# A transformer block on one core: all 32 output-projection groups in one row, and the order of small work around them

## The chip, the core and the metric

The kernel runs on one core of one Trainium2 chip. A core has five engines that run their own instruction streams and wait for each other through semaphores: TensorE (PE; its weight loads are listed as PEld), VectorE (DVE), ScalarE (ACT), GpSimd (POOL) and SyncE (SP), whose queue issues nearly all DMA transfers here. The metric is the time of one execution in microseconds of device time; lower is better. Matmuls write to PSUM, which has eight banks; DVE and ACT read the results out of it.

## What is computed

One pre-LN transformer block on a sequence of 2048 tokens of width 1024: layer norm, sliding-window attention (32 heads of width 32, window 256), output projection with residual, a second layer norm, and an MLP of width 3584 with SiLU, again with residual.

```python
def _A_ref(x, wqkv, wo):
    H = 32; Dh = D // H; W = 256
    q, k, v = ...                       # x @ wqkv, split by head
    scores = jnp.einsum("bhqd,bhkd->bhqk", q, k) * (Dh ** -0.5)
    mask = (idx[:, None] - idx[None, :] >= 0) & (idx[:, None] - idx[None, :] < W)
    p = _softmax(jnp.where(mask[None, None], scores, -1e9))
    o = jnp.einsum("bhqk,bhkd->bhqd", p, v)
    return o.transpose(...).reshape(B, S, D) @ wo

def _B_ref(x, w1, w2):
    return jnp.einsum("bsf,fd->bsd", _silu(jnp.einsum("bsd,df->bsf", x, w1)), w2)

h = x + _A_ref(_layernorm(x), A_wqkv, A_wo)
h2 = h + _B_ref(_layernorm(h), B_w1, B_w2)
```

All inputs are bf16; sums are kept in float32.

## The kernel before

The tokens are cut into four blocks of 512 (`NB` = 4), a block into four tiles of 128. The order of all instructions is written out by hand, and each engine runs its own in that order. The unit of dense work on TensorE is a group: eight matmuls of 128x128 weights against 512 columns that add up in one PSUM bank, the accumulator, which DVE (sometimes ACT) then reads out. While attention is running, three accumulators rotate (`next_acc`, `acc_n`, the first three of `four`); the fourth bank, `o_ps`, holds the outputs of attention, and four more banks, `sc`, hold scores.

The stages, by dense groups:

- Block 0's value groups, then its 16 query and key groups (`qk_group`).
- Blocks 1, 2 and 3: 24 groups each (8 value, 16 query and key), with the first layer norm of the next block between them.
- The row (L691 to L714): 24 groups of the output projection (`wo_group`), two column halves for each of four tiles of blocks 0, 1 and 2.
- The MLP (from L741), for each block 28 groups of the first product (`h1_group`, then `silu` with a tanh on ACT and a multiply on DVE) and then the second product (`mm2`). Block 0's first product holds the remaining eight groups of the output projection, block 3's, one behind each of its groups 7 to 14 (L751).

Attention is not a stage of its own. It is woven into the dense groups by `Attention.between`, which `qk_group`, `v_group` and `wo_group` call ahead of each of their eight matmuls. It counts these calls (`seen`), and at certain counts it issues either a visit (the score matmuls for some heads, with the exponentials on ACT and the causal and window masks on POOL) or a piece (`attn_piece`: 24 matmuls of 128x33 into `o_ps`, L419, then `attn_norm`: a reciprocal, L430, and a multiply, L431, on DVE, which divide by the softmax sums and free `o_ps`). From block 1 on, twelve periods of 48 counts handle two units of four heads each, i and i+1: visits at 4, 20 and 36 counts, pieces at 41, 46, 59 and 76 counts behind the period's start. The pieces at 41 and 46 are the two halves of unit i, and stand five dense matmuls apart in one group. A third visit (`visit(i, 2)`) writes to `sc`, to `o_ps` and to the accumulator of the group before. With the row's first group at count 704, the last period starts in the row's group 10, and its last piece comes in group 19.

When a unit's second half is done, its transposition by DMA into `qT` goes to `late` and is issued on SP at the next group's start (`run_late`). `wo_group` for a block reads `qT` of that block; it adds the residual (`r_in`, six buffers, loaded by `load_res`) on DVE (L285) into one of two buffers `t_out`, and the store of a finished tile to `h_dram` goes to `late` as well. A tile's two adds must wait until the store of the tile two before has left its buffer.

Block 0's second layer norm is made in the row (`ln2_steps(0)`): one load of 1 MB back from `h_dram` (L623, behind group 9), then 16 steps, in this order: four of statistics (two halves L193 and an aggregate L201 each), a first guess and three Newton rounds for the inverse root (L209 to L216), two normalizations (L221), and then transpositions by DMA (L225) and the other two normalizations in turn. One step follows each of groups 11 to 13, and two follow each group from 14 on, until none is left. The first MLP product of block 0 reads all four transpositions.

The row also issues the loads of the MLP's first weights (`load_w1`). The second weights (`load_w2`) are loaded into regions that the attention used: one at the MLP's start, five more in program order behind group 4 of the first product, and the last one behind its end.

At the MLP's start, the banks of `sc` become four more accumulators, so that seven rotate from there on; `acc_n` is set so that the next accumulator is the one that was used longest ago.

Of the kernel before, what the change touches and what calls it, by code (L numbers as in the profile page):

```python
# [47 lines left out]
def kernel(  # L48
# [21 lines left out]
    NB = S // 512  # L70
# [168 lines left out]
    acc_n = [0]  # L239
    acc_banks = [b[:] for b in four]  # L240

    def next_acc():
        acc_n[0] += 1
        return acc_banks[acc_n[0] % len(acc_banks)]
# [24 lines left out]
    def load_res(t):  # L269
        nc.sync.dma_start(out=r_in[t % 6], in_=x2d[t * P:(t + 1) * P, :])  # L270
# [3 lines left out]
    def run_late():  # L274
        while late:
            late.pop(0)()

    def wo_group(b, j, c, between=None):
        acc = next_acc()
        for g in range(G):  # L280
            if between:
                between(g)
            nc.tensor.matmul(acc, lhsT=qT[b][:, g, j * P:(j + 1) * P], rhs=wo[:, g, c * 512:(c + 1) * 512],  # L283
                             start=(g == 0), stop=(g == G - 1))
        nc.vector.tensor_tensor(out=t_out[j % 2][:, c * 512:(c + 1) * 512], in0=acc,  # L285
                                in1=r_in[(b * 4 + j) % 6][:, c * 512:(c + 1) * 512], op=ALU.add)
        if c == 1:
            late.append(lambda: nc.sync.dma_start(out=h_dram[(b * 4 + j) * P:(b * 4 + j + 1) * P, :], in_=t_out[j % 2]))
# [88 lines left out]
    def scores_0(g, odd):  # L377

        q0 = odd * P
        parts = [  # L380
            (odd, 0, q0, q0 + 320, 0), (odd, 1, q0, q0 + 384, 0),
            (odd + 2, 0, q0 + 256, 448, 320), (odd + 2, 1, q0 + 320, 448, 384),
        ]
        if odd:
            parts = [(a, h, f, min(t, 512), c) for a, h, f, t, c in parts[:2]] + [
                (3, 0, 384, 512, 320), (3, 1, 448, 512, 384), (2, 0, 448, 512, 448), (2, 1, 448, 512, 448)]
        for step in range(0, len(parts), 2):
            for hh in range(4):
                for t, half, qa, qb, col in parts[step:step + 2]:
                    r0 = hh * DH  # L390
                    k0 = t * P + half * 64
                    nc.tensor.matmul(  # L392
                        sc[half * 64:half * 64 + 64, hh, col:col + qb - qa],
                        lhsT=kT[0][r0:r0 + DH, g, k0:k0 + 64],
                        rhs=qT[0][r0:r0 + DH, g, qa:qb],
                        start=True, stop=True, tile_position=(r0, half * 64),
                    )
        e = (ybuf if odd else xbuf)(g)[:, 0:2048].rearrange("p (h q) -> p h q", q=512)
        nc.scalar.activation(out=e[:, :, 0:256], in_=sc[:, :, 0:256], func=ACT.Exp, scale=scale)  # L399
        nc.scalar.activation(out=e[:, :, 320:512], in_=sc[:, :, 256:448], func=ACT.Exp, scale=scale)  # L400
        nc.scalar.activation(out=c_ring[:, (g + 1) % 3, :, 128 + 64 * odd:192 + 64 * odd], in_=sc[:, :, 448:512],
                             func=ACT.Exp, scale=scale)
        select(e[:, :, 0:P], e[:, :, 0:P], True)
        select(e[:, :, 256:384], e[:, :, 320:448], False)
        select(e[:, :, 384:512], e[:, :, 384:512], True)
# [42 lines left out]
    class Attention:  # L448


        def __init__(self):
            self.seen = 0
            self.visits, self.pieces = {}, {}
            for d in range(2 * G):
                self.visits[92 + 10 * d] = lambda d=d: scores_0(d // 2, d % 2)
                self.pieces[(122 + 10 * d, 267, 284)[max(d - 13, 0)]] = (d // 2, d % 2)
            for p in range((NB - 1) * G // 2):
                i, t = G + 2 * p, 256 + 48 * p
                for n in range(3):
                    self.visits[t + 4 + 16 * n] = lambda i=i, n=n: visit(i, n)  # L460
                for n in range(4):
                    self.pieces[t + (41, 46, 59, 76)[n]] = (i + n // 2, n % 2)

        def between(self, kt):
            if self.seen in self.pieces:
                attn_piece(*self.pieces.pop(self.seen))
            if self.seen in self.visits:
                self.visits.pop(self.seen)()
            self.seen += 1
# [80 lines left out]
    for n, step in enumerate(FIRST):  # L550
# [24 lines left out]
        elif len(step) == 4:  # L575
            j, k0, k1, _ = step
# [34 lines left out]
    def ln1_steps(b):  # L611
        st, rs = ln_tiles("a")
        xs = [x_ring[(b % 2) * 4 + j] for j in range(4)]
        steps = [lambda j=j: ln_stats(xs[j], st, j) for j in range(4)]
        steps += rstd_steps(st, rs)
        for j in range(4):
            steps.append(lambda j=j: ln_norm(xs[j], st, rs, j))
        return steps, [lambda j=j: ln_transpose(xs[j], lnT_b[b % 2], j) for j in range(4)]
# [14 lines left out]
    steps = sum(ln1_steps(1), [])  # L633
    for g0 in range(0, G, 4):
        for w in range(2):
            for g in range(g0, g0 + 4):
                run_late()
                n = g0 * 2 + w * 4 + g % 4
# [6 lines left out]
    def load_w1(kt):  # L645
        nc.sync.dma_start(out=w1[:, kt, :], in_=w1_v[:, kt, :])
# [4 lines left out]
    steps, turns = ln1_steps(2)  # L651
# [12 lines left out]
    for b in range(2, NB):  # L664
        dense = [lambda j=j, c=c: v_group(b, j, c, dve, stream.between) for j in range(4) for c in range(2)]
        dense += [lambda w=w, g=g: qk_group(b, w, g, dve, stream.between) for g in range(G) for w in range(2)]
        if b + 1 < NB:
            for j in (0, 2):
                load_x_pair(b + 1, j)
            steps, turns = ln1_steps(b + 1)  # L670
        else:
            steps, turns = [], []
# [16 lines left out]


    dense = []  # L691
    for b in range(NB - 1):
        for j in range(4):
            for c in range(2):
                dense.append((b, j, c))
    for t in range(2, 6):
        load_res(t)
    steps = []
    for n in range(24):
        run_late()  # L700
        if n % 2 == 0 and n >= 2 and n // 2 + 5 < S // P:
            load_res(n // 2 + 5)
        wo_group(*dense[n], stream.between)
        if n == 9:
            steps = ln2_steps(0)
            steps.pop(0)()
        if n in (1, 3, 5, 7, 13):
            load_w1((1, 3, 5, 7, 13).index(n))
        for _ in range(1 if n < 14 else 2):
            if steps and n >= 11:  # L710
                steps.pop(0)()
    assert not stream.visits and not stream.pieces
    while steps:
        steps.pop(0)()  # L714


    def load_w2(i):
        nc.sync.dma_start(out=w2[i], in_=w2_v[:, i * 4:(i + 1) * 4, :])

    ps_sc.__exit__(None, None, None)  # L720
    ps_h1 = ctx.enter_context(tc.tile_pool(name="ps_h1", bufs=1, space=bass.MemoryType.PSUM, reuse_waits="tile"))
    assert acc_n[0] % 3 == 0
    acc_n[0] = 0
    acc_banks += [ps_h1.tile([P, 512], F32, name=f"hacc{i}")[:] for i in range(4)]

    def h1_group(b, ft):
# [16 lines left out]
    for b in range(NB):  # L743
        for ft in range(FT):
            acc = h1_group(b, ft)
            run_late()
            if b == 0 and ft == 4:
                for i in (0, 1, 2, 3, 4):
                    load_w2(i)
            silu(b, acc, ft)  # L750
            if b == 0 and 7 <= ft < 15:  # L751
                j, c = divmod(ft - 7, 2)
                wo_group(NB - 1, j, c)
        load_h(b, 0)
        if b == 0:
            load_w2(6)
        steps = ln2_steps(b + 1) if b + 1 < NB else []
        def mm2(acc, j, c0, c1, first, last):
            for ft in range(first, last):
                nc.tensor.matmul(acc[:, 0:c1 - c0], lhsT=gT[:, ft, j * P:(j + 1) * P], rhs=w2[ft // 4][:, ft % 4, c0:c1],  # L760
                                 start=(ft == 0), stop=(ft == FT - 1))

        for j in range(4):
            if j < 3:
                load_h(b, j + 1)
            cols = [(0, 512), (512, 1024)]
            if b == NB - 1 and j == 3:
                cols = [(0, 512), (512, 768), (768, 896), (896, 1024)]
            accs = [next_acc() for _ in cols]
            early = FT - 4 if b == 0 and j == 0 else 0  # L770
            for acc, (c0, c1) in zip(accs, cols):
                mm2(acc, j, c0, c1, 0, early)
            for acc, (c0, c1) in zip(accs, cols):
                mm2(acc, j, c0, c1, early, FT)
                nc.vector.scalar_tensor_tensor(out=t_out[j % 2][:, c0:c1], in0=acc[:, 0:c1 - c0], scalar=0.5,  # L775
                                               in1=t_in[j % 2][:, c0:c1], op0=ALU.mult, op1=ALU.add)
                nc.sync.dma_start(out=out2d[(b * 4 + j) * P:(b * 4 + j + 1) * P, c0:c1], in_=t_out[j % 2][:, c0:c1])
                for _ in range(3):
                    if steps:
                        steps.pop(0)()  # L780
        while steps:
            steps.pop(0)()
# [30 lines left out]
```

## Time and profile before

| | |
|---|---|
| median of 3 runs | 692.11 us (691.43 to 692.91) |
| the profiled execution | 692.04 us, span 690.3 us |
| granted TensorE clock in the profiled execution | 1.00 |
| PE busy | 684.0 us of the span |
| DVE, ACT, POOL busy | 295.4, 237.7, 155.5 us |

The page's parts are: the busy time of each engine; the span in slices; the DMA queues; the chain of waits that ended last; the costliest groups of instructions; and the DMA issues with their time to landing. In a timeline row stand the start in us, the length in us, engine, line, operation, output<-input, shapes, how many instructions were merged, and in brackets how long the engine had been idle before and what released it. Because matmuls overlap, the rows' lengths are longer than the rate: eight matmuls of 512 columns follow each other faster than each one's own length, so the rate is read from starts. Times of rows count from the span's start.

### The profile page before, as it was taken

What the parts mean: (1) busy time and instruction counts of PE and PEld (TensorE: products, weight loads), DVE (VectorE), ACT (ScalarE), POOL (GpSimd) and SP (SyncE); (2) the same over time, 40 slices, a digit from 0 to 9 for tenths busy, and PEclk for the clock granted to TensorE, in tenths of its full rate; (3) what the DMA queues carried; (4) which work ended last, traced back from release to release, by engine and by line L of the source; (5) the groups of instructions that cost most, each with busy time, mean ns of one, the idle gap of its engine ahead of it and who ended that gap; (6) DMA issues with size and microseconds to landing.
All of it is one profiled execution on the core that took longest, in us unless ns stands there. A gap on an engine that the chain in (4) does not pass through costs nothing.

```text
span 690.3 us, 14586 instructions
## 1 busy us (share of the span) xinstructions
PE 684.0 (99%) x6200; PEld 338.5 (49%) x6200; DVE 295.4 (43%) x616; ACT 237.7 (34%) x412; POOL 155.5 (23%) x247
## 2 busy tenths in 40 slices
PE   9999999999999998999999999999999999999998
PEld 4445555555555554444444444444444444444445
DVE  5287745774444448543316133343133251333111
ACT  7356665666666673121310033300133100233000
POOL 1036656666777665000000000000000000000000
DMA  8824144124531796880123410022300024100010
GB/s 272 261 50 99 20 67 94 26 47 112 161 87 62 224 274 183 244 308 31 31 84 111 88 39 1 0 92 69 84 1 0 24 89 94 39 1 0 31 38 24
DMA packets 77617, 61.50 MB, mean 89 GB/s; under 512 B 52464, under 2 KB 60656, under 8 KB 77552
## 3 DMA queue, kind: packets, MB, share of 16 engines
q1 hardware_dynamic: 77408, 60.31, 31.1%
q8 instruction: 48, 0.79, 0.5%
q10 hardware_dynamic: 144, 0.26, 0.1%
q14 instruction: 17, 0.14, 0.1%
HBM read 39.85 MB, written 8.39 MB: 70 GB/s over the span
## 4 chain that ended last, share of the span: by engine, by line
PE 97%; DVE 1%; DMA 1%; issue 0%; DVEq 0%
PE bank L262 17%; PE hacc L760 16%; PE hacc L729 16%; PE bank L729 12%; PE bank L760 12%; PE bank L252 7%; PE bank L283 6%; PE bank L419 5%; PE sc L360 2%; PE bank L360 1%; PE bank L547 1%; PE hacc L283 1%; DMA h_dram<-r_t 1%; PE sc L392 1%; PE tp L252 1%; PE bank L186 0%
## 5 line engine op out<-in xcount | busy, mean ns | idle before, releaser
L409 POOL TENSOR_SCALAR_AFFINE_SELECT r_e<-r_e 128x512 bf16<-128x512 bf16 x240 | 152.5, 643 | 115.2 <-ACT r_e L399 52.8
L760 PEld LDWEIGHTS <-r_a 128*128 128x128 bf16 x952 | 90.9, 98 | 103.0
L729 PEld LDWEIGHTS <-r_w 128*128 128x128 bf16 x896 | 87.6, 98 | 105.8 <-issue 0.4
L760 PE MATMUL hacc<-r_a 128*128 128x512 bf16 (+2 forms) x560 | 114.7, 366 | 0.0
L729 PE MATMUL hacc<-r_e,r_w 128*128 128x512 bf16 x384 | 85.2, 379 | 0.0
L760 PE MATMUL bank<-r_a 128*128 128x512 bf16 (+1 forms) x392 | 81.3, 368 | 0.0
L738 ACT ACTIVATE r_n<-hacc 128x512 f32<-128x512 f32 x24 | 14.3, 597 | 172.2 <-PE hacc L729 172.2
L262 PEld LDWEIGHTS <-r_w 128*128 128x128 bf16 x512 | 45.4, 97 | 49.4 <-issue 1.0
L729 PE MATMUL bank<-r_e,r_w 128*128 128x512 bf16 x288 | 64.1, 379 | 0.0
L264 DVE CAST r_a<-bank 128x512 bf16<-128x512 f32 x58 | 40.0, 689 | 52.9 <-PE bank L262 33.7
L262 PE MATMUL bank<-r_t,r_w 128*128 128x512 bf16 x256 | 61.3, 379 | 0.0
L262 PE MATMUL bank<-r_w 128*128 128x512 bf16 x256 | 59.4, 379 | 0.0
L419 PEld LDWEIGHTS <-r_e 128*128 128x128 bf16 x1440 | 45.6, 96 | 17.4 <-issue 2.6
L321 ACT ACTIVATE r_e<-sc 128x1536 bf16<-128x1536 f32 x36 | 53.3, 1482 | 0.0
L283 PE MATMUL bank<-r_o,r_a 128*128 128x512 bf16 x224 | 52.6, 379 | 0.0
L419 PE MATMUL bank<-r_a,r_e 128*128 128x33 bf16 x1440 | 46.2, 178 | 1.9 <-DVE r_n L431 1.9
L315 ACT ACTIVATE r_e<-bank 128x512 bf16<-128x512 f32 x48 | 26.1, 597 | 43.7 <-PE bank L360 43.7
L775 DVE SCALAR_TENSOR_TENSOR r_t<-bank,r_t 128x512 bf16<-128x512 f32 (+1 forms) x14 | 9.3, 663 | 67.5 <-PE bank L760 67.5
L283 PEld LDWEIGHTS <-r_a 128*128 128x128 bf16 x256 | 23.3, 97 | 25.8
L775 DVE SCALAR_TENSOR_TENSOR r_t<-hacc,r_t 128x512 bf16<-128x512 f32 (+2 forms) x20 | 13.0, 649 | 52.6 <-PE hacc L760 52.6
L252 PE MATMUL bank<-r_w,r_t 128*128 128x512 bf16 x128 | 30.5, 380 | 0.0
L321 ACT ACTIVATE r_e<-bank 128x384 bf16<-128x384 f32 x48 | 23.8, 495 | 16.8 <-PE bank L360 14.5
(103 smaller groups left out, 573.9 us busy)
## 6 DMA issues: line engine op xcount, KB each, us to landing
r_w<-in_B_w_dram SPq DMA_DIRECT2D x8, 896.0 KB, 5.7
r_a<-in_B_w_dram SPq DMA_DIRECT2D x7, 1024.0 KB, 10.8
r_w<-in_A_wqkv_dram SPq DMA_DIRECT2D x4, 1024.0 KB, 8.5
h_dram<-r_t SPq DMA_DIRECT2D x16, 256.0 KB, 2.6
r_t<-h_dram SPq DMA_DIRECT2D x16, 256.0 KB, 2.9
out_dram<-r_t SPq DMA_DIRECT2D x31, 128.0 KB, 1.7
r_e<-h_dram SPq DMA_DIRECT2D x3, 1024.0 KB, 5.7
r_o<-in_A_x_dram SPq DMA_DIRECT2D x11, 256.0 KB, 5.2
```

The lines of the kernel that those rows point to most:

```text
L252: nc.tensor.matmul(acc, lhsT=lnT_b[b % 2][:, kt, j * P:(j + 1) * P], rhs=wv[:, kt, c * 512:(c + 1) * 512], start=(kt == 0), stop=(kt == KT ...
L262: nc.tensor.matmul(acc, lhsT=wqk[:, kt, col0:col0 + P], rhs=lnT_b[b % 2][:, kt, :], start=(kt == 0), stop=(kt == KT - 1))
L264: copy(out=(qT, kT)[which][b][:, g, :], in_=acc)
L283: nc.tensor.matmul(acc, lhsT=qT[b][:, g, j * P:(j + 1) * P], rhs=wo[:, g, c * 512:(c + 1) * 512], start=(g == 0), stop=(g == G - 1))
L315: nc.scalar.activation(out=c_ring[:, lo:hi + 1:hi - lo, h, :], in_=four[bank].rearrange("p (n q) -> p n q", q=256), func=ACT.Exp, scale=scale)
L321: nc.scalar.activation(out=tri_of(e)[:, h0:h1, :, 64:256], in_=tri, func=ACT.Exp, scale=scale)
L360: nc.tensor.matmul(bank[half * 64:half * 64 + 64, col:col + qb - qa], lhsT=kT[t // 4][r0:r0 + DH, g, k0:k0 + 64], rhs=qT[b][r0:r0 + DH, g, ...
L409: nc.gpsimd.affine_select(out=dst, in_=src, pattern=[[0, n] for n in dst.shape[1:-1]] + [[sgn, P]], compare_op=ALU.is_ge if upper else ALU ...
L419: nc.tensor.matmul(o_ps[:, qt * 2 + hh, 0:VW], lhsT=chunk_of(i, bank, piece, pair * 2 + hh), rhs=v[:, b * 4 + kt, g * 4 + pair * 2 + hh, : ...
L729: nc.tensor.matmul(acc, lhsT=w1[:, kt, ft * P:(ft + 1) * P], rhs=ln2T[b][:, kt, :], start=(kt == 0), stop=(kt == KT - 1))
L760: nc.tensor.matmul(acc[:, 0:c1 - c0], lhsT=gT[:, ft, j * P:(j + 1) * P], rhs=w2[ft // 4][:, ft % 4, c0:c1], start=(ft == 0), stop=(ft == F ...
L775: nc.vector.scalar_tensor_tensor(out=t_out[j % 2][:, c0:c1], in0=acc[:, 0:c1 - c0], scalar=0.5, in1=t_in[j % 2][:, c0:c1], op0=ALU.mult, o ...
```

## The change

Four things change.

- The row gets all 32 groups of the output projection: block 3's eight come at its end, and no longer stand in block 0's first MLP product. The loads at fixed groups of the row stay where they are.
- The 16 steps of block 0's second layer norm: one follows each of groups 13, 15, 17 and 19, two follow each group from 20 on. The load behind group 9 stays.
- In each period of attention, the second half of unit i comes at 45 counts behind the period's start, not at 46: four dense matmuls lie between the two halves.
- The count of accumulators at the MLP's start is set for 32 groups, so that again the one used longest ago comes next.

```diff
-                    self.pieces[t + (41, 46, 59, 76)[n]] = (i + n // 2, n % 2)
+                    self.pieces[t + (41, 45, 59, 76)[n]] = (i + n // 2, n % 2)
...
     dense = []
-    for b in range(NB - 1):
+    for b in range(NB):
         for j in range(4):
             for c in range(2):
                 dense.append((b, j, c))
...
-    for n in range(24):
+    for n in range(32):
         run_late()
...
-        for _ in range(1 if n < 14 else 2):
-            if steps and n >= 11:
+        for _ in range(n % 2 if n < 20 else 2):
+            if steps and n >= 13:
                 steps.pop(0)()
+    assert not steps
     assert not stream.visits and not stream.pieces
-    while steps:
-        steps.pop(0)()
...
-    assert acc_n[0] % 3 == 0
-    acc_n[0] = 0
+    assert acc_n[0] % 3 == 2
+    acc_n[0] = -1
...
             silu(b, acc, ft)
-            if b == 0 and 7 <= ft < 15:
-                j, c = divmod(ft - 7, 2)
-                wo_group(NB - 1, j, c)
```

## The prediction

> **What bounds the kernel now.** I read the page first, then the busy times of four stretches, then the table of who waited for whom from 225 to 300 us, and last the timeline around every wait of TensorE found there.
>
> ```profile
> span 690.3 us, 14586 instructions
> PE 684.0 (99%) x6200; PEld 338.5 (49%) x6200; DVE 295.4 (43%) x616; ACT 237.7 (34%) x412; POOL 155.5 (23%) x247
> PE 97%; DVE 1%; DMA 1%; issue 0%; DVEq 0%
> ```
>
> TensorE (PE) sets the end almost alone; only small holes in its stream can be won, or new ones made. The stretches (length, then busy time of PE, PEld, DVE, ACT, POOL, then clock):
>
> ```profile
> 241.90:256.81 14.91, 14.91 (x274) 8.43 (x272) 6.58 (x15) 9.99 (x20) 10.05 (x16) 1.00 0.89 271
> 256.81:274.06 17.25, 14.82 (x226) 8.16 (x225) 13.60 (x36) 8.53 (x16) 10.06 (x16) 1.00 0.69 199
> 274.06:286.76 12.70, 12.70 (x102) 6.31 (x101) 7.93 (x18) 0.00 (x0) 0.00 (x0) 1.00 0.92 238
> 286.76:348.87 62.11, 62.11 (x289) 28.18 (x289) 24.79 (x36) 16.12 (x27) 0.00 (x0) 1.00 0.36 127
> ```
>
> The last stretch is block 0's first MLP product with the eight projection groups in it: 36 groups of 8 matmuls, 62.11 / 288 = 0.2157 us each, and no hole. The first is one whole period of the attention schedule (48 dense matmuls, three score visits, four attention pieces): 14.91 us, no hole either. The second is the last period, which has one visit fewer and yet takes 17.25. The wait table names its holes:
>
> ```profile
> PE bank L419 <- DVE r_n L431: 1.9, 1, 1.9
> PE bank L360 <- DVE r_t L285: 0.3, 1, 0.3
> ```
>
> How this place should look, from one period earlier: the third visit (L360), then four dense matmuls and one, a piece (L419, 24 small matmuls), five dense, the second piece, with VectorE's reciprocal and multiply (L430, L431) between the pieces.
>
> ```profile
> 249.30 0.43 PE L360 MATMUL sc<-r_a 32*64 32x320 bf16 x24
> ...
> 249.88 1.25 PE L283 MATMUL bank<-r_o,r_a 128*128 128x512 bf16 x5
> ...
> 250.97 0.76 PE L419 MATMUL bank<-r_a,r_e 128*128 128x33 bf16 x24
> ...
> 251.57 1.24 PE L283 MATMUL bank<-r_o,r_a 128*128 128x512 bf16 x5
> 251.83 0.21 DVE L430 RECIPROCAL recip<-bank 128x8 f32<-128x8 f32 x1
> 252.07 0.42 DVE L431 TENSOR_TENSOR r_n<-bank,recip 128x256 bf16<-128x256 f32 x1
> ...
> 252.65 0.76 PE L419 MATMUL bank<-r_a,r_e 128*128 128x33 bf16 x24
> ```
>
> And how it looks in the last period:
>
> ```profile
> 262.15 0.69 DVE L285 TENSOR_TENSOR r_t<-bank,r_a 128x512 bf16<-128x512 f32 x1 [1.05 <-DMA h_dram<-r_t]
> ...
> 262.76 1.28 DVE L193 BATCH_NORM_STATS2 ln_st<-r_a 128x6 f32<-128x512 bf16 x2
> ...
> 264.20 0.43 PE L360 MATMUL sc<-r_a 32*64 32x320 bf16 x24
> 264.20 0.16 DVE L430 RECIPROCAL recip<-bank 128x8 f32<-128x8 f32 x1
> 264.39 0.42 DVE L431 TENSOR_TENSOR r_n<-bank,recip 128x256 bf16<-128x256 f32 x1
> 264.74 0.68 DVE L285 TENSOR_TENSOR r_t<-bank,r_a 128x512 bf16<-128x512 f32 x1
> ...
> 265.80 1.25 PE L283 MATMUL bank<-r_o,r_a 128*128 128x512 bf16 x5
> ...
> 266.89 0.76 PE L419 MATMUL bank<-r_a,r_e 128*128 128x33 bf16 x24
> ...
> 267.54 1.27 DVE L193 BATCH_NORM_STATS2 ln_st<-r_a 128x6 f32<-128x512 bf16 x2
> ...
> 269.95 0.20 DVE L430 RECIPROCAL recip<-bank 128x8 f32<-128x8 f32 x1
> 270.18 0.42 DVE L431 TENSOR_TENSOR r_n<-bank,recip 128x256 bf16<-128x256 f32 x1
> ...
> 270.65 0.75 PE L419 MATMUL bank<-r_a,r_e 128*128 128x33 bf16 x24 [1.92 <-DVE r_n L431]
> ```
>
> The visit takes 265.80 - 264.20 = 1.60 us here and 249.88 - 249.30 = 0.58 there: 1.02 lost. The two pieces are 270.65 - 266.89 = 3.76 apart here, 252.65 - 250.97 = 1.68 there: 2.08 lost. Together 3.10 us. Both times TensorE waits for a small VectorE operation queued behind statistics of block 0's second layer norm: two of 0.64 us and an aggregate before the reciprocal at 264.20, and the same with the first Newton guess before the one at 269.95.
>
> **The change part by part.**
>
> *The layer-norm steps spread out.* Before, one step stood behind each of groups 11 to 13 and two behind each from 14; now one behind 13, 15, 17, 19 and two from 20 to 25. I replay VectorE with the rows' durations. Group 12's residual add still cannot start before 262.15: its row says that it waited 1.05 us for a DMA, the store of the tile whose buffer it takes, and the statistics were done by then. The reciprocal follows at 262.76 (where the statistics stood), multiply to 263.42, group 13's add 263.5 to 264.2. The visit at 264.20 touches the two banks that these free only after its first 24 matmuls, about 0.24 us in, so it runs in 0.58: a margin of some 0.2 us. Then the first statistics, 264.2 to 265.7, group 14's add until 266.6, and the piece, now at 265.87, has its reciprocal free to start at 266.73 with nothing ahead of it. The guess and Newton steps come in groups 20 and 21, after the last piece (group 19). Gain 3.10; bounds: nothing if the whole of both holes returned, 3.10 at most, since regular periods hold no wait. I take 3.0, leaving 0.1 for the thin margin at the visit.
>
> The steps then weigh on groups 20 to 25. With the add at 0.69, the guess at about 0.85, a Newton round at 0.6 with its gaps and two normalizations at 0.54 each, VectorE needs up to 1.9 us a group against TensorE's 8 x 0.2157 = 1.73. By group 23 it is about 1.3 us behind. Three accumulators rotate, so an add may be two groups (3.45 us) late before TensorE stops. No piece or visit is left that would wait. Cost nothing under that cover; without it, 1.3.
>
> *The second piece at 45 instead of 46.* Now only four dense matmuls lie between the pieces of a pair, and one more follows. The small matmuls take 251.57 - 250.97 = 0.60, so the second piece arrives at 0.60 + 4 x 0.2157 = 1.46 after the first instead of 1.68. It overwrites the same accumulator, so it waits for the multiply.
>
> ```profile
> 101.84 0.76 PE L419 MATMUL bank<-r_a,r_e 128*128 128x33 bf16 x24
> 102.95 0.42 DVE L431 TENSOR_TENSOR r_n<-bank,recip 128x256 bf16<-128x256 f32 x1
> 103.52 0.76 PE L419 MATMUL bank<-r_a,r_e 128*128 128x33 bf16 x24
> ```
>
> ```profile
> 116.75 0.76 PE L419 MATMUL bank<-r_a,r_e 128*128 128x33 bf16 x24
> ...
> 118.01 0.42 DVE L431 TENSOR_TENSOR r_n<-bank,recip 128x256 bf16<-128x256 f32 x1
> ...
> 118.49 0.75 PE L419 MATMUL bank<-r_a,r_e 128*128 128x33 bf16 x24
> ```
>
> In the first pair the multiply ends 1.53 after the piece's start, in the one quoted from 250.97 at 1.52; eight more are alike. The pair at 116.75 shows the price of a late one: multiply done at 1.68, second piece 0.06 later, at 1.74. So a regular pair is ready at 1.52 + 0.06 = 1.58 and waits 1.58 - 1.46 = 0.12, eleven times (the last pair, replayed above, is now regular too): 1.32. The pair at 116.75 loses the whole shifted matmul, 0.22. Together 1.5 us. Bounds: 0 if something hides the wait, and 12 x 0.2157 = 2.6 if each pair loses the shifted matmul whole. I take 1.5, being nearest to rows that show both the arrival and the release. Nothing is hidden by it: behind the waiting matmul stands all of TensorE's queue, and regular periods have no later wait in which it could vanish.
>
> [...]
>
> *The eight groups moved.* The same 64 matmuls leave a stretch at 0.2157 us each and join the row's end, where the matmuls between 278.94 and 286.76 ran without a hole too (window 274.06 to 286.76, PE busy all of it). Cost nothing, bounds -0.1 and +0.5. Their adds, stores and loads keep their number: 16 stores and the same residual loads, of which groups 14 to 20 now bring tiles 12 to 15 at the same places as before. The rotation of accumulators shifts by one but keeps its distance. The tanh and multiply behind block 0's first product lose their neighbours; blocks 1 to 3 run that way already.
>
> *What is queued on SP.*
>
> ```profile
> 280.79 1.21 SPq L439 DMA_TRANSPOSE r_a<-r_n  x1
> ...
> 283.18 1.23 SPq L225 DMA_TRANSPOSE r_a<-r_a  x1
> ```
>
> ```profile
> r_a<-in_B_w_dram SPq DMA_DIRECT2D x7, 1024.0 KB, 10.8
> ...
> r_a<-r_n SPq DMA_TRANSPOSE x32, 2.7
> ```
>
> Group 24 reads what the last attention transposition writes. Issued here at 280.79, landing 2.7 later, it will go out about 4 us earlier (3 from the holes, 1 since no layer-norm transposition is ahead of it); group 24 now starts near 283.8: cover over 3 us. The layer norm's last transposition, here at 283.18 and 3.6 us before its reader, moves to about 289, with the MLP starting at 286.76 + 13.8 - 3.0 = 297.5 (both on the rows' old clock, without the 1.5 by which all of it shifts): cover improves. Second-product weights are issued behind the row's last store, so some 10 us later, about 299 to 307, and have until 346; six of them at 10.8 each would not fit one after another, but here they were issued within 8 us and the stretch to 348.87 moved its data at 36% of the DMA engines. Nothing for any of these.
>
> Sum against the profiled execution: 692.04 (span 690.3 and 1.7 around it) - 3.0 + 1.5 = 690.5. The median of the three runs is 692.11, 0.07 above that execution: 690.6, or 0.22% less.
>
> **Rivals.**
>
> *The whole gain is kept:* the shifted second piece costs nothing, because the release reaches TensorE before the arrival I computed. For it: ten of twelve pairs show no wait now. Against: 1.58 is a sum of two rows' numbers and lies after 1.46. Time 692.1 - 3.0 = 689.1.
>
> *The hole only moves:* the store that group 12's add waits for still lands late, the margin of 0.2 us at the visit is gone, and about half of the 3.1 returns behind the first statistics. Then -1.5 + 1.5: 692.1. Against it is that no statistic stands before the add any more.
>
> *Slower, by the second piece:* with four matmuls between, VectorE often reaches the reciprocal late, as at 116.75 where a cast was ahead of it. Its place is the twelve pairs. At 0.25 us a pair the gain is used up (12 x 0.25 = 3.0); from 0.37 the kernel is slower by over 1.4. At 0.45 each: 692.1 - 3.0 + 5.4 = 694.5. Against: VectorE's order is the same and ten pairs are ready at the same 1.52 to 1.53.
>
> **How the numbers follow.** The forecast of 690.6 gets 0.55, the kept gain 0.15, the moved hole 0.2, the slower rival 0.1. 0.2%, about what a measurement here can tell from no change, is 1.4 us. The forecast lies just past it, so of its 0.55 I count 0.38 as faster and 0.17 as the same; with the kept gain, faster 0.53; with the moved hole, the same 0.35; slower 0.12, a little of the moved hole being there. The range, 688.9 to 692.5, runs from the kept gain to just above the moved hole; the forecast's own is 690.0 to 691.3.
>
> **What would show it.** Right: no wait of a piece near 1.9 us and no visit of 1.60 in the last period, which shrinks to about 14.3; in every pair 1.58 between the two pieces, with waits of 0.12 for the multiply, and a period of 15.03 instead of 14.91; the MLP starting 1.5 us earlier than 286.76 + 13.8. Wrong: pairs 1.46 apart with no wait, a visit still stretched, a hole in groups 20 to 31, a wait for a transposition or for weights at the start of either product, or a clock under 1.00.

## The result, and the profile after

The changed kernel takes 689.75 us (median of six executions, 689.51 to 690.50) against 692.75 us for the kernel before in the same comparison: a ratio of 0.9958, with a 95% interval of 0.9944 to 0.9971. It is faster by about 2.9 us; 690.6 and a gain of 1.5 were forecast. The direction and the places are as predicted, the size is about double.

The page of the changed kernel:

```profile
span 688.3 us, 14482 instructions
PE 674.4 (98%) x6099; PEld 338.1 (49%) x6200; DVE 296.0 (43%) x616; ACT 237.8 (35%) x412; POOL 155.4 (23%) x247
PE 97%; issue 2%; DMA 1%; DVE 0%; SPq 0%; ACT 0%; ACTq 0%; DVEq 0%
```

PE's busy time is lower only because 101 matmul records are missing here (6099 of 6200); the span is 2.0 us shorter than the profiled execution of before. The stretches of the changed kernel are one regular period, the last one, the rest of the row, and block 0's first product; their busy times fall short of their lengths by such missing records:

```profile
242.82:257.84 15.02, 14.48 (x269) 8.43 (x272) 6.66 (x15) 9.99 (x20) 10.05 (x16) 1.00 0.85 279
257.84:272.10 14.26, 13.88 (x222) 7.95 (x224) 9.12 (x21) 8.53 (x16) 10.04 (x16) 1.00 0.82 226
272.10:298.73 26.63, 26.47 (x164) 12.74 (x166) 17.54 (x41) 0.00 (x0) 0.00 (x0) 1.00 0.62 153
298.73:347.10 48.37, 48.11 (x221) 21.95 (x224) 19.26 (x28) 16.12 (x27) 0.00 (x0) 1.00 0.39 142
```

The regular period has grown from 14.91 to 15.02 us, and the last one has shrunk from 17.25 to 14.26. Its timeline shows why:

```profile
262.53 0.69 DVE L285 TENSOR_TENSOR r_t<-bank,r_a 128x512 bf16<-128x512 f32 x1 [2.12 <-DMA h_dram<-r_t]
...
263.67 0.21 DVE L430 RECIPROCAL recip<-bank 128x8 f32<-128x8 f32 x1 [0.45 <-PE bank L419]
...
264.48 0.69 DVE L285 TENSOR_TENSOR r_t<-bank,r_a 128x512 bf16<-128x512 f32 x1
265.08 1.28 DVE L193 BATCH_NORM_STATS2 ln_st<-r_a 128x6 f32<-128x512 bf16 x2
265.23 0.43 PE L360 MATMUL sc<-r_a 32*64 32x320 bf16 x24
...
266.04 1.03 PE L283 MATMUL bank<-r_o,r_a 128*128 128x512 bf16 x4 [0.16 <-issue]
...
266.90 0.76 PE L419 MATMUL bank<-r_a,r_e 128*128 128x33 bf16 x24
...
268.01 0.42 DVE L431 TENSOR_TENSOR r_n<-bank,recip 128x256 bf16<-128x256 f32 x1
268.48 0.75 PE L419 MATMUL bank<-r_a,r_e 128*128 128x33 bf16 x24
```

The residual add still waits for its store, 2.12 us now. But no statistics stand between that add, the reciprocal and the next add (264.48) any more; the first come behind them, at 265.08. So the visit starts at 265.23 and the next dense matmuls follow as in a regular period (the first record of the five, one of the missing ones, would stand near 265.8). The two pieces are 268.48 - 266.90 = 1.58 us apart instead of 3.76.

### The profile page after: what moved, and what is told of

Its sections match the earlier page's. It is cut to its first block, busy times and chain, and to the rows that moved or that the text cites. A ratio compares the mean times of both kernels' runs of the same rounds, so it can differ in the third digit from the quotient of the medians.

```text
span 688.3 us, 14482 instructions
## 1 busy us (share of the span) xinstructions
PE 674.4 (98%) x6099; PEld 338.1 (49%) x6200; DVE 296.0 (43%) x616; ACT 237.8 (35%) x412; POOL 155.4 (23%) x247
## 4 chain that ended last, share of the span: by engine, by line
PE 97%; issue 2%; DMA 1%; DVE 0%; SPq 0%; ACT 0%; ACTq 0%; DVEq 0%
PE hacc L728 16%; PE bank L262 16%; PE hacc L756 15%; PE bank L756 13%; PE bank L728 12%; PE bank L283 8%; PE bank L252 6%; PE bank L419 5%; PE sc L360 2%; PE bank L360 1%; PE bank L547 1%; PE sc L392 1%; DMA r_w<-in_A_wqkv_dram 1%; PE tp L252 1%; ACT r_e L321 0%
## 5 line engine op out<-in xcount | busy, mean ns | idle before, releaser
L756 PE MATMUL hacc<-r_a 128*128 128x512 bf16 (+2 forms) x523 | 103.2, 356 | 0.5
L756 PE MATMUL bank<-r_a 128*128 128x512 bf16 x412 | 91.4, 379 | 0.5
L262 PE MATMUL bank<-r_t,r_w 128*128 128x512 bf16 x236 | 57.1, 379 | 2.6 <-issue 2.2
L262 PE MATMUL bank<-r_w 128*128 128x512 bf16 x240 | 56.4, 379 | 1.9 <-issue 1.6
L283 PE MATMUL bank<-r_o,r_a 128*128 128x512 bf16 x242 | 56.4, 379 | 1.5 <-issue 1.1
L737 ACT ACTIVATE r_n<-bank 128x512 f32<-128x512 f32 x18 | 10.7, 597 | 117.0 <-PE bank L728 117.0
L771 DVE SCALAR_TENSOR_TENSOR r_t<-bank,r_t 128x512 bf16<-128x512 f32 x15 | 10.3, 684 | 66.6 <-PE bank L756 66.6
L252 PE MATMUL bank<-r_w,r_t 128*128 128x512 bf16 x118 | 28.9, 379 | 1.1 <-issue 0.8
```

Source lines behind the costliest of these rows:

```text
L252: nc.tensor.matmul(acc, lhsT=lnT_b[b % 2][:, kt, j * P:(j + 1) * P], rhs=wv[:, kt, c * 512:(c + 1) * 512], start=(kt == 0), stop=(kt == KT ...
L262: nc.tensor.matmul(acc, lhsT=wqk[:, kt, col0:col0 + P], rhs=lnT_b[b % 2][:, kt, :], start=(kt == 0), stop=(kt == KT - 1))
L737: nc.scalar.activation(out=th, in_=acc, func=ACT.Tanh, scale=0.5)
```

## The experiments

**The kernel before, once more.** No edit.

> The kernel before, once more, for a second profile of its last attention period. Theory A (the hole in that period is a race of small VectorE operations against transfers and differs from execution to execution): the period that took 17.25 us takes another length, anywhere from 16.5 to 19, and the execution's time moves with it; every other period stays at 14.91. Rival (the spread of the times comes from the head or the tail of the kernel): the period is again 17.2 to 17.3.

Measured: 693.24 us, ratio 0.9999 (0.9986 to 1.0012). This profiled execution took 693.77 us, and its last period is another one: 19.67 us from 256.17 to 275.84, longer than the 16.5 to 19 that were expected. Timeline, then three stretches of 2 us (the granted clock is third from the end):

```profile
260.83 1.29 DVE L193 BATCH_NORM_STATS2 ln_st<-r_a 128x6 f32<-128x512 bf16 x2 [2.09 <-DMA r_a<-h_dram]
...
262.33 0.69 DVE L285 TENSOR_TENSOR r_t<-bank,r_a 128x512 bf16<-128x512 f32 x1
...
263.56 0.43 PE L360 MATMUL sc<-r_a 32*64 32x320 bf16 x24
...
265.05 0.32 PE L360 MATMUL bank<-r_a 32*64 32x320 bf16 x2 [1.06 <-DVE r_n L431]
...
265.64 0.41 PE L360 MATMUL bank<-r_a 32*64 32x320 bf16 x10 [0.27 <-DVE r_t L285]
265.98 1.25 PE L283 MATMUL bank<-r_o,r_a 128*128 128x512 bf16 x5
...
270.83 0.78 PE L419 MATMUL bank<-r_a,r_e 128*128 128x33 bf16 x24 [1.91 <-DVE r_n L431]
271.45 4.56 PE L283 MATMUL bank<-r_o,r_a 128*128 128x512 bf16 x13
```

```profile
270.00:272.00 2.00, 1.17 (x26) 0.87 (x26) 1.06 (x5) 0.00 (x0) 1.41 (x3) 0.82 0.00 0
272.00:274.00 2.00, 2.00 (x7) 0.62 (x5) 1.68 (x7) 0.00 (x0) 0.00 (x0) 0.50 0.25 52
274.00:276.00 2.00, 2.00 (x15) 0.91 (x14) 0.76 (x3) 0.00 (x0) 0.00 (x0) 0.82 0.56 173
```

Here the 1 MB load, issued at 253.75, landed 6.99 us later, so the first statistics began at 260.83 (259.57 in the first profile) and stood ahead of the add too. The visit takes 265.98 - 263.56 = 2.42 us, 1.84 more than a regular one; the pieces lose 2.08 as before. And behind the second hole the granted clock falls to 0.50, and the weight loads of the dense matmuls start 0.43 us apart there (271.83, 272.26, 272.69) instead of 0.2157. An estimate that counts the three stretches as made of 1.00 and 0.50 alone gives (1 - 0.82) x 2 / 0.5 + 2 + 0.72 = 3.4 us at half rate, in which TensorE loses half of that, 1.7 us. Holes and clock together cost 1.84 + 2.08 + 1.7 = 5.6 us here, not 3.1. Of 58 executions of the kernel before, timed on two chips beside the first eight runs, 42 have a mean clock under 1.00. Their medians are 693.69 on one chip (21 executions) and 694.56 on the other (21); those with 1.00 have 692.92 and 692.53 (8 each). The execution profiled first was one of the minority.

**The second piece at 45 alone.**

```diff
-                    self.pieces[t + (41, 46, 59, 76)[n]] = (i + n // 2, n % 2)
+                    self.pieces[t + (41, 45, 59, 76)[n]] = (i + n // 2, n % 2)
```

> The kernel before with the second piece at 45 alone. Theory A: the two pieces of each regular pair stand 1.58 us apart, periods take 15.02 instead of 14.91, and the hole in the last period stays and is longer by one dense matmul (0.22): 1.5 to 1.7 us slower than before, near 694. Rival (the earlier piece costs nothing or helps): within 0.3 us of before.

Measured: 695.24 us, ratio 1.0024 (1.0014 to 1.0034), 1.7 us slower. In its trace every regular pair is 1.58 to 1.59 us apart and the late one 1.74; the last period still waits:

```profile
PE bank L419 <- DVE r_n L431: 2.1, 1, 2.1
PE bank L360 <- DVE r_n L431: 0.9, 1, 0.9
PE bank L360 <- DVE r_t L285: 0.3, 1, 0.3
```

The 2.1 is the old 1.9 and the dense matmul that no longer stands ahead of the piece. The clock is not the reason for the 1.7: among executions with a lowered clock alone, the medians are 695.31 here (11 of 12) and 693.69 for the kernel before on the same chip, 1.6 apart. So this part of the change costs what was forecast.

**The eight groups moved alone**, with the layer-norm steps and the second piece as before; the diff is against the changed kernel.

```diff
-                    self.pieces[t + (41, 45, 59, 76)[n]] = (i + n // 2, n % 2)
+                    self.pieces[t + (41, 46, 59, 76)[n]] = (i + n // 2, n % 2)
...
-        for _ in range(n % 2 if n < 20 else 2):
-            if steps and n >= 13:
+        for _ in range(1 if n < 14 else 2):
+            if steps and n >= 11:
```

> The eight groups moved into the row, with the layer-norm steps where the kernel before has them and the second piece at 46. Theory A: the move is worth nothing by itself; the last period still has its hole of 3 us, and the time is within 0.5 us of before, 692 to 693. Rival (the eight groups cost something between the first products): 1.5 to 3 us faster, though the hole is still there.

Measured: 693.55 us, ratio 0.9999 (0.9984 to 1.0013). Nine of its twelve executions have a clock under 1.00, and in its trace TensorE still waits 0.94, 0.28 and 1.91 us in the last period. The move by itself is worth nothing that could be told from zero; the interval reaches about 1 us to each side.

**The changed kernel with the second piece at 46.**

```diff
-                    self.pieces[t + (41, 45, 59, 76)[n]] = (i + n // 2, n % 2)
+                    self.pieces[t + (41, 46, 59, 76)[n]] = (i + n // 2, n % 2)
```

> The changed kernel with the second piece back at 46. Theory A: pairs stand 1.68 apart again without a wait, except the one behind a late cast (1.74), periods take 14.91, and the kernel is 1.4 to 1.5 us faster than the changed one: 688.3, 4.4 us under the kernel before. Rival (45 is what makes the last period run without its hole): the pair in the last period waits again for 1 to 2 us, and the time is at or above 689.7.

Measured: 688.93 us, ratio 0.9935 (0.9920 to 0.9950). A regular period and the last one:

```profile
241.92:256.82 14.90, 14.90 (x273) 8.44 (x272) 6.58 (x15) 9.98 (x19) 10.01 (x16) 1.00 0.87 242
256.82:270.99 14.17, 14.17 (x226) 7.96 (x225) 8.74 (x20) 8.55 (x16) 10.01 (x16) 1.00 0.96 275
```

Both run without a hole, so 45 is not what closes the last period's; in this trace the last pair is 1.68 apart like the regular ones.

**The layer-norm steps held back alone**, in the 24 groups that the row had before.

```diff
-        for _ in range(1 if n < 14 else 2):
-            if steps and n >= 11:
+        for _ in range(n % 2 if n < 20 else 3):
+            if steps and n >= 13:
```

> The kernel before (24 groups in the row, second piece at 46) with the layer-norm steps held back alone: one behind groups 13, 15, 17, 19, three behind each of 20 to 23. Theory A: the last period runs without a hole (14.2 us, clock 1.00), but the last transpositions of the layer norm go out only some 3 us ahead of the MLP's first matmul plus their landing of 3.4, so TensorE waits 4 to 7 us there, and the clock falls behind that wait: 693 to 697. So the eight groups are what covers the delay. Rival (the transpositions land in time): the time of the changed kernel at 46, 688.9.

Measured: 697.46 us, ratio 1.0062 (1.0045 to 1.0080), just above the stated 693 to 697. The hole of the last period is gone (TensorE is busy 26.36 of the 27.00 us from 255 to 282, and the table of waits names no other engine or transfer there), and a longer one stands at the MLP's first matmul, with a granted clock of 0.70 over it and 0.50 behind it:

```profile
290.61 4.99 PE L729 MATMUL bank<-r_a,r_w 128*128 128x512 bf16 x16 [6.59 <-DMA r_a<-r_a]
```

```profile
255.00:282.00 27.00, 26.36 (x366) 14.70 (x357) 18.35 (x45) 9.99 (x18) 10.49 (x17) 1.00 0.74 211
284.00:290.60 6.60, 0.01 (x1) 0.02 (x1) 1.70 (x4) 0.00 (x0) 0.00 (x0) 0.70 0.96 199
290.60:292.60 2.00, 1.99 (x5) 0.70 (x6) 0.00 (x0) 0.00 (x0) 0.00 (x0) 0.50 0.48 46
292.60:294.60 2.00, 2.00 (x9) 0.81 (x8) 0.07 (x1) 0.60 (x1) 0.00 (x0) 0.79 1.01 387
```

By the same count that is (1 - 0.70) x 6.6 / 0.5 + 2 + (1 - 0.79) x 2 / 0.5 = 6.8 us at half rate, twice the 3.4 of the kernel before; only 2.8 of them, behind the wait, slow any matmul.

So the eight groups pay as cover: 13.8 us of matmuls that need none of the layer norm, behind which its last transpositions can land. Whether some other order of the steps would do without them in 24 groups was not tried.

**One hole of known size.** Two runs put statistics steps behind group 14 of the changed kernel at 46, ahead of the reciprocal that the last period's second piece waits for: two steps in the first, three in the second.

```diff
-        for _ in range(n % 2 if n < 20 else 2):
+        for _ in range({13: 1, 14: 2, 17: 1}.get(n, 0) if n < 20 else 2):
```

```diff
-        for _ in range(n % 2 if n < 20 else 2):
+        for _ in range({13: 1, 14: 3}.get(n, 0) if n < 20 else 2):
```

> The changed kernel with the second piece at 46, and two of the statistics steps behind group 14, right ahead of the reciprocal that the last period's second piece waits for: one hole of about 2.8 us. [...] Rival (any hole of over 2 us lowers the clock): 0.5 for about 3 us behind it and 1.6 us more, 693.3.

> As before, with three statistics steps there: one hole of about 4.3 us. Theory A: the clock falls to 0.5 for about 3 us behind it, and the time is 688.9 + 4.3 + 1.6 = 694.8. Rival (it takes two holes one after the other): the clock stays at 1.00, 693.2.

With two steps: 692.80 us, ratio 0.9984 (0.9972 to 0.9996). The profiled execution kept its clock at 1.00; its add was late, so it also has small waits at the visit:

```profile
265.91 0.32 PE L360 MATMUL bank<-r_a 32*64 32x320 bf16 x2 [0.47 <-DVE r_n L431]
...
266.51 0.41 PE L360 MATMUL bank<-r_a 32*64 32x320 bf16 x10 [0.27 <-DVE r_t L285]
...
272.09 0.75 PE L419 MATMUL bank<-r_a,r_e 128*128 128x33 bf16 x24 [2.31 <-DVE r_n L431]
```

The add, at 264.59 here, is taken to have waited for its store, which went out at 258.38, 6.2 us earlier: in the traces of before and of the changed kernel the row of this add names the store (1.05 and 2.12 us), while here it names an exponential on ACT. No statistics stood ahead of it. Of this kernel's ten executions four have a mean clock of 1.00 (median 691.50, near 688.9 + 2.8 = 691.7, the hole alone) and six a lower one (693.07, near the rival's 693.3). The rival does not hold as it was put: with this hole the mean clock was lower in six executions and stayed at 1.00 in four. With three steps: 695.05 us for 694.8 expected, ratio 1.0018 (1.0005 to 1.0031), and all ten executions have the lower clock, after one wait of 3.70 us:

```profile
270.93 0.82 PE L419 MATMUL bank<-r_a,r_e 128*128 128x33 bf16 x24 [3.70 <-DVE r_n L431]
```

```profile
271.00:273.00 2.00, 1.78 (x27) 1.15 (x28) 0.98 (x3) 0.00 (x0) 0.00 (x0) 0.53 0.04 8
273.00:275.00 2.00, 2.00 (x8) 0.68 (x6) 0.34 (x1) 0.00 (x0) 0.00 (x0) 0.62 0.37 66
```

That is (0.47 + 0.38) x 2 / 0.5 = 3.4 us at half rate again, by the same count. One hole was enough here.

**The second piece at 44.**

```diff
-                    self.pieces[t + (41, 45, 59, 76)[n]] = (i + n // 2, n % 2)
+                    self.pieces[t + (41, 44, 59, 76)[n]] = (i + n // 2, n % 2)
```

> The changed kernel with the second piece at 44: three dense matmuls between the halves. Theory A (the second piece cannot start before 1.58 us behind the first): pairs stay 1.58 apart with a wait of 0.33, periods take 15.23, and the kernel is 12 x 0.216 = 2.6 us slower than the changed one: 692.3. Rival (the multiply starts earlier too): less than 1 us slower.

Measured: 693.15 us, ratio 0.9990 (0.9977 to 1.0003). Against the changed kernel's ratio of 0.9958 that is 0.0032 x 693 = 2.2 us more, for 2.6 expected; the 0.4 us between the two lie within the intervals. In the traces, the time from the first pair to the MLP's first matmul is 199.66 us here and 197.04 in the changed kernel, 2.62 more. A pair and the next period's first piece:

```profile
209.28 0.76 PE L419 MATMUL bank<-r_a,r_e 128*128 128x33 bf16 x24
...
210.86 0.75 PE L419 MATMUL bank<-r_a,r_e 128*128 128x33 bf16 x24 [0.17 <-DVE r_n L431]
...
224.52 0.76 PE L419 MATMUL bank<-r_a,r_e 128*128 128x33 bf16 x24
```

The pieces stay 1.58 apart with three dense matmuls between them as with four, and the period is 224.52 - 209.28 = 15.24: the matmul taken out of the gap is paid behind it. The bracket gives a wait of 0.17 us, not the expected 0.33, because a dense matmul's row is 0.38 us long while the next one starts 0.22 behind it: the first 0.16 of the wait lie inside that row. For the same reason the wait of 0.12 at 45 stands in no bracket and no table, and only the starts show it.

**45 and 46 on one chip.** The changed kernel and its 46 variant again.

> The changed kernel once more, on the same chip as the next run. Theory A: no hole, so a granted clock of 1.00 in every execution, and a narrow spread of times; about 3 us under the kernel before.

> The changed kernel with the second piece at 46, beside the changed kernel on one chip. Theory A: 10 regular pairs by 0.10 to 0.12 us, the last pair the same, and the late one by 0.22: 1.4 to 1.5 us under the changed kernel, clock 1.00 in every execution. Rival (its lead came from another chip): within 0.5 us of the changed kernel.

Measured: 690.03 us (689.93 to 690.96), ratio 0.9955 (0.9942 to 0.9968), and 688.92 us (688.56 to 691.05), ratio 0.9942 (0.9926 to 0.9957). The medians are 1.1 us apart for 1.4 to 1.5 expected, and the intervals overlap; with the two ratios of 0.9935 and 0.9942 against 0.9958 and 0.9955, the 46 variant is the best kernel of this study. The traces say the same: from the first pair to the MLP's first matmul the changed kernel takes 197.04 and 197.06 us, the 46 variant 195.59 and 195.84. All eleven executions have a clock of 1.00.

## Why the prediction was right, and where its size was off

*The layer-norm steps spread out, 3.0 gained.* Right in place and mechanism. Between the two recorded executions, which both kept the full clock, the visit and the pair gave back 1.02 and 1.96 (3.76 - 1.58 = 2.18 between the pieces, less the 0.22 of the dense matmul that now stands behind them); without the groups moved this turns into a loss, as the run with the steps held back alone showed. The margin at the visit held in the recorded execution: the add ended at 265.17, and the matmuls that need its bank came at 265.49. That was in part luck. The run with two statistics behind group 14 has the same order up to the visit, and there the late store alone, as read above, made the visit wait 0.47 and 0.27 us. So the race with the store is still in the changed kernel; what it no longer meets are the statistics. What failed is the size of this term: it was read from one execution and bounded by its 3.10. In another execution, where the 1 MB load landed later, the same holes cost 3.9 us, and 5.6 with the clock behind them. The replay's load on VectorE was off too, without harm: by its own terms group 20 takes 0.69 + 0.85 + 0.6 = 2.14 us, not up to 1.9, while the changed kernel's rows show 1.64 (adds at 280.10 and 281.74), and no add is more than about 0.3 us late there, where 1.3 was forecast.

*No term for the clock.* This was wrong. The four stretches showed 1.00 because that one execution kept it; in 42 of 58 it did not. In the second trace of the kernel before the clock fell to 0.50 though no single wait was over 1.91 us: once, behind a few waits in one place. The 0.12 us waits at 45 did not lower it: all eleven executions of the changed kernel have 1.00. So the clock spoke for this change, while the prediction named it only as a sign of being wrong.

*The second piece at 45, 1.5 lost.* Right: 1.7 measured alone, with pairs at 1.58 as worked out, and 1.1 to 1.5 won back by taking it out.

*The eight groups, nothing.* Right: 0.9999 alone, and no hole in the row's end. That they are also what lets the steps move was treated only as improved cover. With the steps held back and the second piece at 46, 697.46 us without them stand against 688.93 with them, so this is their worth here.

*Transpositions, loads and stores, nothing.* Right: the changed kernel's table of waits from 225 to 300 us has no wait of TensorE for another engine or a transfer (the waits at 45 are too short for it, as said above).

*The sum.* From one recorded execution to the other the MLP starts at 298.57 instead of 286.76 + 13.8 = 300.56. 0.31 of these 2.0 us stands before the first pair (101.84 before, 101.53 after) and has nothing to do with the change; 1.7 is left for 1.5 forecast. The other 1.3 us or so between the medians fit what the recorded execution of before did not show: longer holes and the lowered clock. This split is inferred, not shown, since the six executions behind the median of 692.75 have no clock on record.

Of the rivals, the kept gain (689.1) came nearest in time but for another reason, since 45 did cost its 1.5. The hole did not move in the recorded execution, though a smaller one of that kind stood at the visit in the run just named, and VectorE was not later at the other pairs.

## What to carry to other kernels

Where a small operation of one engine releases the bounding engine, count what the same queue may hold ahead of it, and keep long steps that nobody waits for behind the last such release; then find independent work that covers their later end. Read a hole's cost from several executions, with the mean clock of each beside its time: a race with a transfer changes from one to the next (17.25 and 19.67 us for the same period here), and an idle time can cost more than its own length, here 1.7 us more through the clock. A wait of 0.1 us in a loop that otherwise has none is paid each time round, and undoing it here was worth 1.1 to 1.5 us, at least as much as the smaller of the two holes.

## What the runs showed of the hardware that was not expected

The granted clock fell to 0.50 after waits of 1.06, 0.27 and 1.91 us, all between 263.99 and 270.83; after one of 2.31 with 0.74 close before it, it did not in the execution that was recorded, but six of that kernel's ten executions had a lower mean clock; after one of 3.70 it fell in the recorded execution, to 0.53 and 0.62 in two stretches of 2 us, and the mean clock was lower in ten of ten. By the count above, the stretch at half rate was 3.4 us long in two of the traces, and 6.8 where TensorE had waited 6.59. Why the clock falls in one execution of a kernel and not in another was not shown. The holes are not quite the same each time: TensorE's waits in the last period add up to 2.43 us (the first profile of before) and 3.05 (two steps) in traces that kept the clock, and to 3.13 (the eight groups alone), 3.24 (before again), 3.33 (45 alone) and 3.70 (three steps) in traces that lost it. So the larger sums lost it in these six traces, but the nearest two are only 0.08 apart, and no run varied the sum by itself. The longest single wait does not part them: the clock was kept with one of 2.31 and lost with one of 1.91.
